# One value tile's load cut by partitions: 112, 8 and 8 rows in place of 128

## The chip, the cores and the metric

The kernel runs on one core of a Trainium2 chip. The metric is the device time of one execution in microseconds (us), given as the median of several runs; lower is better. The core has five engines that run side by side: TensorE (PE, with its weight loads PEld), VectorE (DVE), ScalarE (ACT), GpSimd (POOL) and SyncE (SP), which here only issues transfers. Sixteen DMA engines carry the data between the main memory (HBM) and the on-chip memory (SBUF), which has 128 partitions, called rows here.

## What is computed

One decoding step of a transformer block for four sequences: attention over a cached set of 4096 keys and values in 32 heads of 128, and a gated feed-forward part, both modulated by a conditioning vector `c`. Cut to what matters:

```python
q = (h @ wq).reshape(B, 1, 32, 128).transpose(0, 2, 1, 3)      # B = 4, one query per head
scores = einsum('bhqd,bhkd->bhqk', q, k_cache) * 128 ** -0.5   # k_cache: 4 x 32 x 4096 x 128, bf16
p = softmax(scores, axis=-1)
o = einsum('bhqk,bhkd->bhqd', p, v_cache)                      # v_cache: as k_cache
x = x + ga * (o.transpose(0, 2, 1, 3).reshape(B, 1, 4096) @ wo)
h = layernorm(x) * (1 + cb) + sb
x = x + gb * gmlp(h, w_in, w_sp, b_sp, w_out)
```

The two caches hold 134 MB each and are read once; all weights together are a few per cent of that. Each cached number is used for one query only.

## The kernel before

**Tiles.** The work on the caches is cut into NT = 32 tiles, each of one batch entry and four heads (HQ = 4). A key tile and a value tile have the same shape: 128 partitions, and in each of them 128 positions (NJ) of 128 numbers (DH), bf16. That is 32 KB a partition, contiguous in HBM (`kv_view`, L91 to L94), and 4096 KB a tile. Partition 32q + r holds a stretch of positions of head q.

**Buffers.** Key tiles have two buffers named `kt`, value tiles two named `vt`. The last value tile (index L = 31) takes a `kt` buffer and is loaded in four cuts along the positions (`TAIL`), and the last key tile in two, so that the work at the end can begin on a part of the tile. All other tiles are loaded by one DMA each. Loads are issued by SP in program order (`load`, L101); a load waits on SP until the tile that had the buffer before has been used.

**The loop** (L81 to L504), iteration i: VectorE multiplies key tile i in place by the query, in two halves (`mult`, L279); TensorE sums the products over the 128 numbers with an identity matrix into `red` (`reduce_d`, L285), and VectorE finishes the sum (`sum8`, L294). The softmax of tile i-1 (`scores`: L303 to L317, on VectorE and ScalarE) and its normalisation (`norm_r`, `norm_a`, `norm_b`: L325, L332, L345) run beside it. The product of probabilities and values for tile i-2 is `pv(i - 2)` (L354, 32 matmuls that read the whole value tile), and the output of tile i-3 is picked out of PSUM (`o_pick`, `o_cols`, `o_scale`: L362, L366, L380, L396).

**The order of loads.** The schedule is written out by hand. Before the loop SP issues `wm_sb`, `wq_sb`, key tiles 0 and 1, and value tile 0. In iteration i it issues key tile i+2 after the second half of `reduce_d(i)`, and value tile i after `pv(i - 2)`, which has just freed its buffer. Value tile 16 is thus issued in iteration 16, stands in SP's queue between key tiles 18 and 19, and is read by `pv(16)` in iteration 18. In iteration 30 SP issues the last value tile's four cuts, `win_sb` and `wout_sb`.

**The tail** (L506 to L645): the last tiles' outputs, the projection with `wo`, the layer norm (which ends in `hT2`, L562), the gate matmuls on `win_sb` (L585), the activation and the product `zz` (L601), the matmuls on `wout_sb` (L608), and the result's way out.

ScalarE issues four tiny loads on a queue of its own: `c_sb` and `x_sb` (4 partitions of 1 KB each, at the start) and the two numbers of `sp_t` (one partition each, in iteration 2).

Of the kernel before, what the change touches and what calls it, by code (L numbers as in the profile page):

```python
# [16 lines left out]
KC = 64  # L17
RD = 8
TAIL = (64, 32, 16, 16)


@with_exitstack
def kernel(
# [16 lines left out]
    nc = tc.nc  # L40
    P = 128
# [7 lines left out]
    NJ = SK * HQ // P  # L49
# [3 lines left out]
    G = 4  # L53
    assert DH == P and R == 32 and NJ % KC == 0 and KC * RD == 512 and sum(TAIL) == NJ
    assert G * HQ <= R and G * DH == 512 and NQ % G == 0
    att_scale = float(DH) ** -0.5
    LN_EPS = 1e-5
    L = NT - 1
# [32 lines left out]
    def kv_view(cache, i):  # L91
        g, b = divmod(i, B)
        v = cache[b, g * HQ:(g + 1) * HQ].rearrange("h s d -> (h s) d")
        return v.rearrange("(p n) d -> p n d", p=P)  # L94

    kts, vts = {}, {}

    def load(dst, src, cuts):
        n0 = 0
        for n in cuts:  # L100
            nc.sync.dma_start(out=dst[:, n0:n0 + n, :], in_=src[:, n0:n0 + n, :])  # L101
            n0 += n
# [6 lines left out]
    def load_v(i):  # L109

        vts[i] = kvp.tile([P, NJ, DH], BF16, name="kt" if i == L else "vt", bufs=2)
        load(vts[i], kv_view(A_v_cache, i), TAIL if i == L else (NJ,))

    load_k(0)
    load_k(1)
    load_v(0)

    ident_bf = consts.tile([P, P], BF16, name="ident_bf")
# [21 lines left out]
        out=sel32, in_=ident_f.rearrange("p (q r) -> p r q", r=R), axis=AX.X, op=ALU.add  # L140
# [10 lines left out]
    for g in range(G):  # L151
        nc.vector.tensor_reduce(out=selg[:, g:g + 1], in_=idr[:, g], axis=AX.XY, op=ALU.add)
    nc.vector.tensor_reduce(
        out=sel4, in_=ident_f.rearrange("p (c b) -> p b c", b=B), axis=AX.X, op=ALU.add
# [39 lines left out]
    def normed(pool, src, name, then=None, last=None):  # L194
# [24 lines left out]
        out=sg, in0=cx, scalar1=-60.0, scalar2=-1.0, op0=ALU.max, op1=ALU.mult  # L219
# [6 lines left out]
    def mod_cols(s0, n, dst, m0=0, blocks=False):  # L226
# [21 lines left out]
        out=hs, in0=modA[:, DJ:2 * DJ, :], scalar=1.0, in1=xn, op0=ALU.add, op1=ALU.mult  # L248
# [137 lines left out]
    def o_last(i, part):  # L386
        if part == 0:
            st[i, "op"] = psum.tile([P, 2, 2], F32, name="qps", bufs=1)
        for k in range(sum(TAIL[:part]), sum(TAIL[:part + 1])):
            nc.tensor.matmul(  # L390
# [44 lines left out]
    for i in range(NT):  # L435
# [29 lines left out]
        if i == 0:  # L465
            load_v(1)
        elif 2 <= i < L:
            load_v(i)
        if i == 2:
# [13 lines left out]
                out=wo_sb, in_=A_wo[0:hl].rearrange("(t p r) n -> p t r n", p=P, r=2)  # L483
            )
            nc.sync.dma_start(out=wo_last, in_=A_wo[hl:H * DH].rearrange("(q p) n -> p q n", p=P))
        if i == 5:
# [4 lines left out]
                out=gwT, in0=gsT, scalar1=spf[:, 0:1], scalar2=None, op0=ALU.mult  # L491
            )
            nc.vector.tensor_scalar(
                out=gsT, in0=gsT, scalar1=spf[:, 1:2], scalar2=None, op0=ALU.mult
# [34 lines left out]
    def sums():  # L529
# [22 lines left out]
        out=nv2, in0=mq2[:, 0:1], scalar=mq2[:, 0:1], in1=mq2[:, 1:2],  # L552
# [7 lines left out]
        out=hl, in0=xs, scalar=mq2[:, 0:1], in1=cbT[:, :, BL], op0=ALU.subtract, op1=ALU.mult  # L560
    )
    nc.vector.scalar_tensor_tensor(  # L562
        out=hT2[:, :, BL], in0=hl, scalar=rsl, in1=sbT[:, :, BL], op0=ALU.mult, op1=ALU.add
# [4 lines left out]
        out=x1m, in0=x1[:, :, :, None].to_broadcast([P, DJ, B, HQ]),  # L568
# [11 lines left out]
    def gate(h):  # L580
# [21 lines left out]
        out=zz.rearrange("p f g b -> p g b f"), in0=z1[:, None].to_broadcast([P, 2, B, NH]),  # L602
# [3 lines left out]
    for j in range(DJ):  # L606
# [7 lines left out]
        out=mq3, in_=ps3.rearrange("p (g b f) -> p g b f", g=2, b=B), axis=AX.X, op=ALU.add  # L614
# [4 lines left out]
        out=rs3, in0=mq3[:, 1], scalar=LN_EPS, in1=rs3, op0=ALU.add, op1=ALU.subtract  # L619
# [3 lines left out]
        out=g8[:, :, 0, :], in0=gwT.rearrange("p j b -> p b j"), scalar=-1.0,  # L623
# [6 lines left out]
        out=t3[:, :, 2, :], in0=yb[:, :, 0, :], in1=gsT.rearrange("p j b -> p b j"), op=ALU.mult  # L630
    )
    nc.vector.tensor_tensor(
        out=g8[:, :, 0:2, :], in0=g8[:, :, 0:2, :],
# [5 lines left out]
        out=tt, in_=t3.rearrange("p b g j -> p b j g"), axis=AX.X, op=ALU.add  # L639
# [36 lines left out]
```

## Time and profile before

| | |
|---|---|
| time, median of 3 runs | 670.07 us (669.81 to 670.64) |
| the profiled execution's own time | 671.33 us |
| its span, first to last instruction | 669.5 us |
| mean granted TensorE clock | 0.828 |
| busy: PE, DVE, ACT | 403.3 us (60%), 421.1 us (63%), 85.0 us (13%) |
| moved by DMA | 283.18 MB, mean 423 GB/s |
| the chain that ended last | DMA 58%, DVE 28%, PE 13% |
| DVE waiting for key tiles (L279) | 190.7 us in 29 waits, the longest 17.3 us |

The page counts an engine as busy while it executes; the chain follows the work that ended last back from the end, at each step to what released it. A load's time is told from its issue on SP to its landing, so waiting in the queue behind earlier loads is part of it: 22.6 us for a key tile in the median, 30.3 us for a value tile. A load has landed when its semaphore has had sixteen increments, which the trace keeps one by one. It also keeps the single packets that the DMA engines moved, with queue, size, start and duration, but not the number of the DMA engine.

### The profile page before, as it was taken

The page shows a single profiled execution, that of the slowest core. Times are in us where ns is not written, and L with a number is a line of the kernel's source. Part 1 is how long each engine was busy: PE and PEld are TensorE (multiplying, and loading weights), DVE is VectorE, ACT ScalarE, POOL GpSimd, SP SyncE. Part 2 cuts the span into 40 slices and gives each one's busy share as a digit, 9 for nine tenths or more (in the row PEclk, how much of TensorE's full clock was granted, in tenths as well). Part 3 has the DMA queues.
Part 4 walks back from the last instruction along what each step waited for, and adds up shares of the span by engine and source line. Part 5 has one row for each costly group of instructions (what it writes and reads, how often), then busy time and mean ns, then how long its engine had stood idle before and what let it go on. Part 6 is the DMA issues. An engine that isn't in the chain of part 4 may idle for free.

```text
span 669.5 us, 7043 instructions
## 1 busy us (share of the span) xinstructions
PE 403.3 (60%) x2920; PEld 181.8 (27%) x2920; DVE 421.1 (63%) x614; ACT 85.0 (13%) x278; POOL 3.8 (1%) x17
## 2 busy tenths in 40 slices
PE   1185886365676576557655664675565467555666
PEld 1032432122232232223222222232222233222325
DVE  3186494765666776666677665567766666776833
ACT  1011111110111111001111100111111011111112
POOL 1000000000000000000000000000000000000000
PEclk9999877678888777898877689878778897877975
DMA  9999999999999999999999999999999999999994
GB/s 376 437 426 435 400 404 418 433 439 428 430 433 434 435 432 431 432 435 434 430 433 431 434 434 433 430 431 432 437 432 435 426 436 433 435 434 422 435 422 198
DMA packets 13555, 283.18 MB, mean 423 GB/s; under 512 B 1228, under 2 KB 2644, under 8 KB 4692
## 3 DMA queue, kind: packets, MB, share of 16 engines
q1 hardware_dynamic: 13504, 282.73, 98.6%
q8 instruction: 23, 0.38, 0.2%
q14 instruction: 8, 0.07, 0.0%
q10 hardware_dynamic: 20, 0.01, 0.0%
HBM read 282.73 MB, written 0.00 MB: 422 GB/s over the span
## 4 chain that ended last, share of the span: by engine, by line
DMA 58%; DVE 28%; PE 13%; issue 1%; SPq 0%; ACT 0%; DVEq 0%
DMA kt<-in_A_k_cache_dram 52%; DVE kt L279 20%; PE red L285 11%; DMA win_sb<-in_B_w_in_dram 5%; DVE osb L366 2%; DVE S L294 1%; DVE osb L362 1%; DVE mrow L303 1%; PE ops L354 1%; DVE rz L345 1%; DVE mt L307 0%; PE qps L265 0%; DVE nM L309 0%; DVE mb L305 0%; DVE nM L310 0%
## 5 line engine op out<-in xcount | busy, mean ns | idle before, releaser
L285 PE MATMUL red<-kt,ident_bf 128*128 128x512 bf16 x1024 | 302.3, 461 | 234.7 <-DVE kt L279 234.7
L279 DVE TENSOR_TENSOR kt<-kt,qbc 128x8192 bf16<-128x8192 bf16 x64 | 282.8, 4420 | 191.7 <-DMA kt<-in_A_k_cache_dram 190.7
L285 PEld LDWEIGHTS <-ident_bf 128*128 128x128 bf16 x1024 | 116.3, 114 | 408.7 <-issue 284.9
L317 ACT ACTIVATE pbd<-S,nM 32x128 bf16<-32x128 f32 x128 | 73.8, 576 | 504.9 <-DVE nM L310 463.6
L354 PE MATMUL ops<-vt,pbd 128*16 128x512 bf16 x992 | 60.7, 387 | 0.2 <-DMA vt<-in_A_v_cache_dram 0.2
L294 DVE TENSOR_REDUCE S<-red 128x64 f32<-128x512 f32 x64 | 43.7, 682 | 6.3 <-PE red L285 6.3
L366 DVE SCALAR_TENSOR_TENSOR osb<-ops,selg,osb 128x128 f32<-128x128 f32 x93 | 32.6, 351 | 3.3
L317 ACT ACTIVATION_READ_ACCUMULATOR pbd<-S,nM 32x1 f32 x128 | 32.0, 250 | 0.0
L354 PEld LDWEIGHTS <-pbd 128*16 128x16 bf16 x992 | 22.5, 90 | 23.4 <-issue 1.8
L265 PE MATMUL qps<-wq_sb,hTb 128*32 128x512 bf16 x128 | 9.2, 412 | 9.2 <-DMA wq_sb<-in_A_wq_dram 8.5
L332 PEld LDWEIGHTS sm<-rsb,ones_f 128*128 128x128 f32 x64 | 12.3, 194 | 4.5
L362 DVE TENSOR_SCALAR osb<-ops,selg 128x128 f32<-128x128 f32 x31 | 10.8, 348 | 4.3 <-PE ops L354 3.6
L380 PEld LDWEIGHTS sm<-sel,osb 128*64 128x64 f32 x224 | 9.2, 138 | 11.9 <-issue 11.4
L380 PE MATMUL sm<-sel,osb 128*64 128x2 f32 x224 | 11.6, 205 | 0.0
L269 ACT CAST qbc<-qps 128x512 bf16<-128x512 f32 x8 | 4.7, 586 | 48.3 <-PE qps L265 48.3
L303 DVE TENSOR_REDUCE mrow<-S 128x1 f32<-128x128 f32 x32 | 9.2, 286 | 1.1
L345 DVE RECIPROCAL rz<-sm 64x2 f32<-64x2 f32 x56 | 9.1, 163 | 0.4
L332 PE MATMUL sm<-rsb,ones_f 128*128 128x4 f32 x64 | 9.3, 215 | 0.0
L325 DVE TENSOR_SCALAR rsb<-mask,rs 128x4 f32<-128x4 f32 x32 | 7.1, 223 | 2.4 <-ACT pbd L317 2.4
L307 DVE STREAM_TRANSPOSE mt<-mb 128x32 f32<-128x32 f32 x32 | 6.8, 212 | 1.1
L265 PEld LDWEIGHTS <-hTb 128*32 128x32 bf16 x128 | 3.0, 99 | 13.3 <-issue 10.6
L309 DVE TENSOR_REDUCE nM<-mt 128x1 f32<-128x32 f32 x32 | 6.0, 186 | 1.1
(125 smaller groups left out, 84.4 us busy)
## 6 DMA issues: line engine op xcount, KB each, us to landing
kt<-in_A_k_cache_dram SPq DMA_DIRECT2D x31, 4096.0 KB, 22.6
vt<-in_A_v_cache_dram SPq DMA_DIRECT2D x31, 4096.0 KB, 30.3
wq_sb<-in_A_wq_dram SPq DMA_DIRECT2D x1, 4096.0 KB
kt<-in_A_k_cache_dram SPq DMA_DIRECT2D x2, 2048.0 KB, 20.3
wo_sb<-in_A_wo_dram SPq DMA_DIRECT2D x1, 3584.0 KB, 29.3
wm_sb<-in_w_mod_dram SPq DMA_DIRECT2D x1, 3072.0 KB, 10.4
kt<-in_A_v_cache_dram SPq DMA_DIRECT2D x1, 2048.0 KB
win_sb<-in_B_w_in_dram SPq DMA_DIRECT2D x1, 1792.0 KB, 33.9
```

Of the source, the lines that this page charges most:

```text
L265: nc.tensor.matmul(qp[R * q:R * (q + 1)], lhsT=hTb[:, k, b, :], rhs=wq_v[:, k, gs, q, :], start=(k == 0), stop=(k == DJ - 1), tile_positio ...
L279: nc.vector.tensor_tensor(out=kt, in0=kt, in1=bc(qbc[:, g, b, :], KC), op=ALU.mult)
L285: nc.tensor.matmul(red, lhsT=ident_bf, rhs=kt[:, :, m * RD:(m + 1) * RD], start=(m == 0), stop=(m == DH // RD - 1),)
L294: nc.vector.tensor_reduce(out=st[i, "S"][:, kc * KC:(kc + 1) * KC], in_=st.pop((i, "red", kc)), axis=AX.X, op=ALU.add,)
L303: nc.vector.tensor_reduce(out=mrow, in_=S, axis=AX.X, op=ALU.max)
L317: nc.scalar.activation(out=pbd[r, :, q], in_=S[r, :], func=AF.Exp, bias=nM[r, :], scale=att_scale, accum_out=rs[r, :],)
L332: nc.tensor.matmul(z, lhsT=ones_f, rhs=st.pop((i, "rsb")), start=True, stop=True)
L345: nc.vector.reciprocal(out=rz[h, 0, :], in_=z[h, a:HQ:2])
L354: nc.tensor.matmul(opss[i % 2][g:g + G * HQ], lhsT=pbds[i % 3][:, n, :], rhs=vts[i][:, n, :], start=(m < 4), stop=(m >= NJ // G - 4), tile ...
L362: nc.vector.tensor_scalar(out=osb, in0=ops[:, 0, :], scalar1=selg[:, 0:1], scalar2=None, op0=ALU.mult)
L366: nc.vector.scalar_tensor_tensor(out=osb, in0=ops[:, g, :], scalar=selg[:, g:g + 1], in1=osb, op0=ALU.mult, op1=ALU.add,)
L380: nc.tensor.matmul(op[64 * a:64 * (a + 1), r, :], lhsT=osb[:, r:P:2], rhs=sel4[:, a:HQ:2], start=True, stop=True, tile_position=(0, 64 * a),)
```

## The change

`load_v` gets a case for the tiles in a new list `FEW`, which holds tile 16 alone. That tile is loaded by three DMAs in place of one: partitions 0 to 111, 112 to 119, and 120 to 127, in this order, on the same queue and at the same place. Buffer, source, bytes, and all that reads the tile are as before.

```diff
 TAIL = (64, 32, 16, 16)
+
+FEW = (16,)
...
     def load_v(i):
 
         vts[i] = kvp.tile([P, NJ, DH], BF16, name="kt" if i == L else "vt", bufs=2)
-        load(vts[i], kv_view(A_v_cache, i), TAIL if i == L else (NJ,))
+        src = kv_view(A_v_cache, i)
+        if i in FEW:
+            for p0, p1 in ((0, P - 16), (P - 16, P - 8), (P - 8, P)):
+                nc.sync.dma_start(out=vts[i][p0:p1], in_=src[p0:p1])
+        else:
+            load(vts[i], src, TAIL if i == L else (NJ,))
```

## The prediction

> **What bounds the kernel now.** I read the page from the top: the slices, then the DMA queues, then the chain that ended last, and after that the timeline around the changed tile and at the end.
>
> ```profile
> DMA  9999999999999999999999999999999999999994
> ...
> q1 hardware_dynamic: 13504, 282.73, 98.6%
> q8 instruction: 23, 0.38, 0.2%
> q14 instruction: 8, 0.07, 0.0%
> q10 hardware_dynamic: 20, 0.01, 0.0%
> ```
>
> The transfer engines are full in 39 of 40 slices, and one queue, SP's (q1), fills 98.6% of them. 8.39 MB (a key and a value tile of 4096 KB each) at the 432 GB/s of the middle slices take 19.4 us. A tile has 128 rows of 32 KB, and the trace records sixteen arrivals for a load, one for each transfer engine, so an engine moves 8 rows in 9.7 us: 1.21 us a row. The trace's packet records say the same: 8,064 packets of 32 KB, the median 1.213 us. That time holds also where few engines are still at work, so it is an engine's own pace and not a share of a common one.
>
> The chain in order of time shows how this sets the end:
>
> ```profile
> 370.50 23.16 DMA kt<-in_A_k_cache_dram
> 393.69 4.42 DVE kt L279
> ...
> 628.08 33.87 DMA win_sb<-in_B_w_in_dram
> 662.00 1.67 PE red L585 x56
> ```
>
> Every iteration waits for its key tile, and the tail waits for `win_sb`. The compute between fits inside the 19.4 us: VectorE is busy 63%, TensorE 60%. So what counts is when the slowest of the sixteen engines is done.
>
> They are not done together. For `win_sb` the trace has the first arrival at 655.97 us and the others, after it, at 0.0, 0.7, 0.9, 1.3, 2.2, 2.8, 3.1, 3.2, 4.2, 4.4, 4.5, 4.5, 4.9, 5.7 and 6.0 us: eight early engines within 3.1 us, eight late ones up to 6.0. At 49 us the spread was 1.8, at 364 us (value tile 15) 3.1, at 404 us (value tile 17) 4.3. Following each engine by its packets, one 1.21 us after the other, shows why: the 23 instruction fetches of q8 (16 KB each) fall in turn on eight of the engines, and one of them sets its engine back by about 1.4 us (at 42.8 us the packets expected at 42.82 and 44.03 start at 43.77 and 45.45). 23 x 1.4 / 8 = 4 us for each of these eight by the end. The queue is never empty after 111 us, so no engine catches up.
>
> In the tail three loads release the work, all of them by their last arrival:
>
> ```profile
> 657.44 0.51 PEld L390 LDWEIGHTS <-kt 128*128 128x128 bf16 x16 [0.72 <-DMA kt<-in_A_v_cache_dram]
> ...
> 662.00 1.66 PE L585 MATMUL red<-hT,win_sb 128*128 128x4 bf16 x56 [0.68 <-DMA win_sb<-in_B_w_in_dram]
> ...
> 664.35 0.82 PEld L608 LDWEIGHTS <-wout_sb 128*128 128x128 bf16 x28 [0.36 <-DMA wout_sb<-in_B_w_out_dram]
> ```
>
> The computed inputs of the latter two are there at 661.43 (L562) and 664.33 (L601), within 0.6 us of the loads. If the latest engine moves by some time, all three loads do, and the end moves by it in full, both ways.
>
> **The change, part by part.** *Removed:* one issue of 4096 KB, 0.33 us on SP, 8 rows for each engine. *Added:* an issue with 112 rows, which I take as 7 a engine (7 x 16), and two with 8 rows. *Moved:* nothing; the three stand in the place of the one.
>
> ```profile
> 353.15 0.33 SPq L101 DMA_DIRECT2D vt<-in_A_v_cache_dram  x1
> ...
> 370.50 0.33 SPq L101 DMA_DIRECT2D kt<-in_A_k_cache_dram  x1
> ...
> 390.96 1.90 PE L354 MATMUL ops<-vt,pbd 128*16 128x512 bf16 x32
> ...
> 393.69 4.42 DVE L279 TENSOR_TENSOR kt<-kt,qbc 128x8192 bf16<-128x8192 bf16 x1 [6.17 <-DMA kt<-in_A_k_cache_dram]
> ```
>
> *Issues.* Two more at 0.33 us make 0.66 us on SP. SP's next issue is 17 us later and waits for other engines, so 0; without that cover 0.66 us.
>
> *Waits.* The product at L354 waits for three loads in place of one. Tile 16's arrivals cannot be told apart; halfway between those of tiles 15 and 17 its last would be at 384.2, 6.8 us before 390.96. Behind that product on TensorE stands the reduction of the next key tile, which needs the multiply from 393.69 to 398.1; behind it on SP, the load of value tile 18. The product takes 1.9 us, so it may start as late as 396.2 without holding up the reduction: 12 us after the tile's usual arrival. Cost 0 under that cover; beyond it, each microsecond of lateness counts.
>
> *The rows.* This is the term that decides. The loads of `c_sb` and `x_sb` (4 rows of 1 KB) left four packets each on q10, and the two one-row loads of `sp_t` one each: a narrow load uses as many engines as it has rows. So an 8-row part should occupy eight engines with one row each; I assume the same eight for both parts. Their share of the tile is then 7 + 2 rows, that of the other eight 7. The engine that carried the `sp_t` loads and the four that carried `x_sb` show no q8 fetch while I can follow them, which puts the eight in the early group (likely, not certain).
>
> How fast 8 rows are written, the trace does not show; every large load in it fills 128 rows. Bounds for one 8-row part: at the engine's pace, 1.21 us. At the other end the rate goes with the rows filled: 432 GB/s over 128 rows is 3.4 GB/s a row, so 32 KB take 9.7 us, the same as eight rows one after another down a single engine's stream. No row lies near either end (the only narrow loads carry 1 KB rows and are over in 0.05 us a packet), so I take the middle, (1.21 + 9.68) / 2 = 5.44 us.
>
> Sum for the early group: 7 x 1.21 + 2 x 5.44 = 19.4 us in place of 9.7, that is +9.7. Its latest member was 3.1 us behind the first and becomes 12.8; the end was set at 6.0. So +6.8 us: span 676.3 for 669.5. The profiled execution took 671.33 us, 1.8 around its span; on the median of 670.07 it is **676.9 us**. With the bounds: at 1.21 us the early group ends at 3.1 + 1.2 = 4.3, the late one at 6.0 - 1.2 = 4.8, and the end comes 1.2 us earlier, 668.9; at 9.68 us a part the group loses 2 x 9.68 - 1.21 = 18.1 us, ends at 21.2, and the end is 15.2 later, 685.3.
>
> [...]
>
> **Rivals.** *Rebalancing at full pace.* Narrow parts run at 1.21 us a row; eight late engines lose a row and the early ones gain one: -1.2 us, 668.9. For it: an engine's packets take the same time whatever the others do, and the arrivals part into 8 and 8. [...]
> *Wrong side.* The parts fall on the late eight, at full pace: the latest goes from 6.0 to 7.2, +1.2 us, 671.3. This is slower by one row's time; it decides where the fetches and the narrow loads share engines. Against it stand the packets of `x_sb` and `sp_t`.
> *No shift.* The two parts take different eights, or are spread over all sixteen: each engine has 8 rows as before, 670.1. Against it: with one row to each engine, nothing suggests that the queue picks up where it left off.
>
> **How the numbers follow.** Slow narrow parts (671.5 to 685.3 around 676.9, the likeliest's own range) 0.64; rebalancing 0.27; wrong side 0.05; no shift 0.04. This kernel's measurement can tell about 0.2%, 1.3 us. Rebalancing at 1.2 us lies just inside that and falls on either side: 0.15 beyond it, 0.12 within. Faster 0.15; same 0.12 + 0.04 + 0.03 of the wrong side = 0.19; slower 0.64 + 0.02 = 0.66. The range takes in rebalancing with some noise below (668.4) and the forecast up to 683.5, where most of what lies under its bound of 685.3 is in; about 0.08 is left above and 0.03 below.
>
> **What would show it.** In the changed profile: packets of 32 KB that take several times 1.21 us around 380 to 395 us, GB/s well under 430 in that slice, the arrivals of the loads after it 9 to 13 us apart, and TensorE at L354 waiting for the value tile there. If no packet is longer and the last spread of `win_sb` is about 4.8 us, rebalancing holds and my forecast is wrong; 7.2 us is the wrong side; 6.0 no shift. A gain over 1.3 us, or a loss with unchanged arrivals, would show that I have missed a mechanism.

## The result, and the profile after

The changed kernel took 686.34 us in the median of 4 runs (684.30 to 686.94) against 669.97 before: 1.023 times the time, with a 95% interval of 1.021 to 1.025. Slower by 6.8 us was forecast; it is slower by 16.4, outside the range and past the bound of 685.3. The profiled execution took 686.27 us with a span of 684.4, 14.9 over the span before.

The time is lost in one place. The slices of the page, after:

```profile
DMA  9999999999999999999999999999999999999993
GB/s 376 439 429 434 430 402 431 429 428 429 432 443 434 432 431 428 429 432 435 440 432 355 199 372 435 435 432 435 428 430 431 436 431 432 439 432 420 435 425 157
```

A slice is 17.1 us. From 359 to 410 us three slices move 355, 199 and 372 GB/s in place of 432; no slice before or after them shows a loss like it against the kernel before. The share of the DMA engines stays at 9 throughout: they are busy, with packets that take longer. The three slices lack (77 + 233 + 60) x 17.1 = 6.3 MB, which at 432 GB/s are 14.6 us: nearly the whole loss in the span. (The loss in the median is larger, 16.4 us, because the profiled execution of the kernel before, 671.33 us, lay 1.4 us above its median.)

A finer cut, stretches of the same two kernels; the columns after the length are busy time and instructions of each engine, TensorE's clock, the DMA share and GB/s. First before, then after:

```profile
372.00:380.00 8.00, 1.57 (x11) 0.49 (x4) 5.52 (x5) 0.00 (x0) 0.00 (x0) 0.66 1.01 434
386.00:396.00 10.00, 6.09 (x66) 3.17 (x66) 3.83 (x5) 0.00 (x0) 0.00 (x0) 0.95 1.00 431
400.00:408.00 8.00, 5.80 (x30) 2.46 (x28) 6.78 (x10) 2.31 (x8) 0.00 (x0) 0.88 1.01 438
```

```profile
372.00:380.00 8.00, 0.00 (x0) 0.10 (x1) 4.11 (x1) 0.00 (x0) 0.00 (x0) 0.69 0.97 217
386.00:396.00 10.00, 4.99 (x44) 2.79 (x42) 3.04 (x4) 0.00 (x0) 0.00 (x0) 0.98 0.88 161
400.00:408.00 8.00, 3.59 (x32) 1.07 (x32) 0.00 (x0) 0.00 (x0) 0.00 (x0) 0.50 0.99 424
```

There are two slow stretches, and the trace's packets of 32 KB fit them. Up to 368 us they take 1.21 us. Those that start from 370 to 384 us, while the 112-row part is on its way, take about 2.3 us (1.7 to 2.6). Those that start from 384 to 396 us, when the two 8-row parts are under way, take 2.2 to 3.9. From 400 us on it is 1.21 again. What the packets took beyond 1.21 us, added up over the sixteen engines and divided by 16, is 7.1 us for those that start before 384 and 7.4 us for the later ones: two halves. The cut at 384 is a rough one: by the arrivals the 112-row part lands from 386.18 to 394.58 us and the two 8-row parts, eight arrivals each, from 389.88 to 399.88, so late engines are still on the wide part while early ones are on the narrow ones. What each part costs is told apart by the experiments.

The timeline after shows who waits (the multiply is now L286, the product L361, the three loads L117, other loads L103):

```profile
352.06 1.45 SPq L117 DMA_DIRECT2D vt<-in_A_v_cache_dram  x3
...
369.80 0.35 SPq L103 DMA_DIRECT2D kt<-in_A_k_cache_dram  x1
...
375.89 4.43 DVE L286 TENSOR_TENSOR kt<-kt,qbc 128x8192 bf16<-128x8192 bf16 x1 [8.99 <-DMA kt<-in_A_k_cache_dram]
...
400.01 3.59 PE L361 MATMUL ops<-vt,pbd 128*16 128x512 bf16 x32 [7.46 <-DMA vt<-in_A_v_cache_dram]
...
409.29 4.42 DVE L286 TENSOR_TENSOR kt<-kt,qbc 128x8192 bf16<-128x8192 bf16 x1 [20.25 <-DMA kt<-in_A_k_cache_dram]
```

Key tile 19, behind tile 16 in the queue, lands at 409.26 us in place of 393.67, 15.6 later, and VectorE waits 20.25 us for it in place of 6.17. In the chain of waits that one load stands for all of it:

```profile
369.80 39.47 DMA kt<-in_A_k_cache_dram
409.29 4.42 DVE kt L286
```

It was 23.16 us before. At the end `win_sb` arrives last at 676.44 us, 14.5 later. Next to nothing was caught up.

### The profile page after: what moved, and what is told of

Its sections match the earlier page's. It is cut to its first block, busy times and chain, and to the rows that moved or that the text cites. A ratio compares the mean times of both kernels' runs of the same rounds, so it can differ in the third digit from the quotient of the medians.

```text
span 684.4 us, 7047 instructions
## 1 busy us (share of the span) xinstructions
PE 415.7 (61%) x2920; PEld 185.2 (27%) x2920; DVE 421.0 (62%) x614; ACT 85.0 (12%) x278; POOL 3.8 (1%) x17
## 4 chain that ended last, share of the span: by engine, by line
DMA 53%; DVE 30%; PE 15%; issue 1%; ACT 1%; SPq 0%; DVEq 0%
DMA kt<-in_A_k_cache_dram 53%; DVE kt L286 21%; PE red L292 12%; DVE osb L373 3%; DVE S L301 2%; PE ops L361 1%; DVE osb L369 1%; DVE mrow L310 1%; DVE mt L314 1%; DVE rz L352 1%; PE qps L397 0%; DVE nM L316 0%; DVE mb L312 0%; DVE nM L317 0%; PE sm L240 0%
## 5 line engine op out<-in xcount | busy, mean ns | idle before, releaser
L292 PE MATMUL red<-kt,ident_bf 128*128 128x512 bf16 x1024 | 312.8, 474 | 231.3 <-DVE kt L286 231.3
L286 DVE TENSOR_TENSOR kt<-kt,qbc 128x8192 bf16<-128x8192 bf16 x64 | 282.8, 4420 | 207.0 <-DMA kt<-in_A_k_cache_dram 206.1
L292 PEld LDWEIGHTS <-ident_bf 128*128 128x128 bf16 x1024 | 119.2, 117 | 413.4 <-issue 293.6
L361 PE MATMUL ops<-vt,pbd 128*16 128x512 bf16 x992 | 62.4, 396 | 7.5 <-DMA vt<-in_A_v_cache_dram 7.5
L361 PEld LDWEIGHTS <-pbd 128*16 128x16 bf16 x992 | 22.6, 91 | 31.7 <-issue 10.8
```

The costliest lines, as they stand in the source:

```text
L286: nc.vector.tensor_tensor(out=kt, in0=kt, in1=bc(qbc[:, g, b, :], KC), op=ALU.mult)
L292: nc.tensor.matmul(red, lhsT=ident_bf, rhs=kt[:, :, m * RD:(m + 1) * RD], start=(m == 0), stop=(m == DH // RD - 1),)
L361: nc.tensor.matmul(opss[i % 2][g:g + G * HQ], lhsT=pbds[i % 3][:, n, :], rhs=vts[i][:, n, :], start=(m < 4), stop=(m >= NJ // G - 4), tile ...
```

## The experiments

The times stand beside runs of the kernel before on the same chip (670.0 to 670.4 us). As a second measure, closer to the place, I give when key tile 19 has landed (its sixteenth arrival; 393.67 before). In kernels that do not load all of the tile the end mixes in other things: the queue runs dry for a moment (in only8s, strided8 and narrow_low as few as 14, 12 and 14 of the sixteen engines have a packet under way between 370 and 373 us), and in the tail the gate matmuls wait for `hT2` and no longer for `win_sb`. There the landing is the better number.

The expectations weigh four theories, conjectures that the runs are to part. A: engines that write into neighbouring rows at the same time share one engine's pace, so every part that is not the plain 128 rows is slow. B: only the 8-row parts are slow. C: the number of loads costs, with their waits and semaphores. D: the source side costs, where engines read rows that lie next to each other.

**Is it the number of loads?** Three loads too, each of all 128 rows, cut along the positions:

```diff
-            for p0, p1 in ((0, P - 16), (P - 16, P - 8), (P - 8, P)):
-                nc.sync.dma_start(out=vts[i][p0:p1], in_=src[p0:p1])
+            load(vts[i], src, (112, 8, 8))
```

> Tile 16 in three loads too, but each of all 128 rows: 112, 8 and 8 positions of each. Theory A and theory B: no change, 670 +- 1. Theory C (number of loads, three waits at L354, the shifted order of semaphores): about 686, as the changed kernel.

670.33 us, ratio 1.0006 (95% interval 0.9995 to 1.0017); key tile 19 lands at 392.69. Two more issues, two more waits at the product and a shifted order of semaphores cost nothing that can be measured. Theory C is out.

**Which part costs?** First the 112 rows alone:

```diff
-            for p0, p1 in ((0, P - 16), (P - 16, P - 8), (P - 8, P)):
+            for p0, p1 in ((0, P - 16),):
...
     def pv(i):
+        if i in FEW:
+            return
```

> Tile 16 gets its first 112 rows alone; the last 16 rows are not loaded and its product (L354) is left out. Theory A (engines that write into neighbouring rows at the same time share one engine's pace, so every part that is not the plain 128 rows is slow): the 112-row part takes 2.2 to 2.4 us a row as in the changed profile, 7 rows +7.6 us, less the two rows not loaded: 674 to 678 us. Theory B (only the 8-row parts are slow, as the prediction had it): 668 to 670. Theory C (the cost comes with the number of loads, their marks and waits): 668 to 670.

680.94 us, ratio 1.016 (1.013 to 1.019), above even theory A. The stretch of this kernel:

```profile
372.00:380.00 8.00, 0.00 (x0) 0.10 (x1) 4.41 (x2) 0.00 (x0) 0.00 (x0) 0.81 0.95 213
```

Half of the 434 GB/s, with packets of 2.2 to 2.4 us (1.7 to 1.9 in places). Key tile 19 lands at 400.71; with one row less for each engine it would land at 392.5 at full pace, so this part costs 8.2 us. Of the 10.9 us at the end some 2.4 come after the last load: from `win_sb`'s last arrival to the output's issue 6.0 us pass in place of 5.2, and one of the output's sixteen arrivals is 1.6 us behind. Another 6.5 stand at `win_sb`'s arrival (668.43 for 661.95), and the remaining 2 are how far the two profiled executions lie from their medians. Theory B is out: the wide part that the prediction had at full pace is half of the loss.

Then the two 8-row parts alone, with the product left out in the same way:

> Tile 16 gets rows 112 to 119 and 120 to 127 alone; its other 112 rows are not loaded and its product is left out. At an engine's full pace all engines save 7 to 8 rows of 1.21 us and the end comes 9.7 us earlier: 660.3. [...] Theory B: the whole excess of 15 us sits here: 672 to 676. Theory C: 672 to 676.

670.82 us, ratio 1.0009 (0.9997 to 1.0022): leaving out seven eighths of a tile gained nothing, though by the expectation's sum 9.7 us were to be had at full pace (strided8_low below, at nearly full pace, gains 7.0). This lies below the 672 of B and C. Key tile 19 lands at 392.82, and from 372 to 380 us:

```profile
372.00:380.00 8.00, 1.21 (x24) 0.46 (x17) 0.23 (x1) 0.00 (x0) 0.00 (x0) 0.78 0.98 152
```

**Where do the rows have to lie?** The same bytes from the same place, but the eight rows of a part land four rows apart (the edit is shown against only8s):

```diff
-            for p0, p1 in ((P - 16, P - 8), (P - 8, P)):
-                nc.sync.dma_start(out=vts[i][p0:p1], in_=src[p0:p1])
+            for p0, s0 in ((64, P - 16), (96, P - 8)):
+                nc.sync.dma_start(out=vts[i][p0:p0 + 32:4], in_=src[s0:s0 + 8])
```

> As only8s, from the same source rows, but the eight rows of each part land four rows apart (64, 68, ..., 92 and 96, 100, ..., 124). [...] If the cost of a narrow part goes with the number of rows filled, or with where the rows are read from, or with the number of loads: the same as only8s.

667.75 us, key tile 19 at 389.05: faster than only8s by 3.1 us, but packets are still at 1.9 to 2.6 us from 371 to 376. The stretch:

```profile
372.00:380.00 8.00, 1.52 (x32) 0.60 (x21) 3.96 (x1) 0.00 (x0) 0.00 (x0) 0.78 0.91 279
```

Spreading the rows helps, but the time is not that of full pace (660.3 by the expectation of only8s). A conjecture for what is left, which no run had shown at that point: rows 64 to 127 are those into which the late engines write at the same time. That says what to try next: `((0, P - 16), (32, P - 8))` in the loop, rows 0 to 60 in steps of four.

> As strided8, from the same source rows, but the two narrow parts land on rows 0, 4, ..., 28 and 32, 36, ..., 60, which I take to be rows of the early engines themselves; strided8 wrote into rows of the late ones. Theory A (shared rows of the destination make the loss; a path is one engine's pace wide): nobody shares, all packets stay at 1.21 us, 2 to 5 us below strided8's 667.8 (not all the way to 660.3, since the queue runs dry for a while in these kernels). Theory D (the source side, eight engines reading rows that lie next to each other, makes a part of the loss): packets of 2 us and more as in strided8, and its time.

663.38 us, and key tile 19 lands at 384.64, 8.2 us before only8s. The stretch of this kernel:

```profile
372.00:380.00 8.00, 2.34 (x6) 0.94 (x7) 6.60 (x10) 0.48 (x2) 0.00 (x0) 0.81 1.00 430
```

Full rate, in two narrow parts of eight rows, beside 152 GB/s for the same bytes in neighbouring rows. From 368 to 380 us five packets of 151 are long (1.6 to 2.7 us); all five start within 2 us of an instruction fetch at 370.10 (in the kernel before two are long beside the fetches at that place), and the other 146 take 1.21 to 1.23. So neither the narrowness nor the source of these parts costs anything that shows, only where the rows land. That rows 0 to 60 go at full pace and rows 64 to 124 do not, with the step the same, fits narrow parts that run on the engines which write rows 0 to 63 in a plain load; the traces have no engine numbers, so this is inferred.

**Does the source play a part?** One plain load of 128 rows from source rows 28 KB apart; the values are then not those of the tile:

```diff
+            flat = A_v_cache[i % B, (i // B) * HQ:(i // B + 1) * HQ].rearrange("h s d -> (h s d)")
+            rows = bass.AP(tensor=flat.tensor, offset=flat.offset, ap=[[112 * DH, P], [1, NJ * DH]])
+            nc.sync.dma_start(out=vts[i].rearrange("p n d -> p (n d)"), in_=rows)
```

> Tile 16 in one plain load of 128 rows whose source rows start 28 KB apart in place of 32 (they overlap, so the values are not the tile's; the bytes moved are the same). Theory A: no change, 670 +- 1. Theory D: packets longer than 1.21 us in this tile and a later end.

670.24 us, ratio 0.9996 (0.998 to 1.001), packets at 1.21 us. Another step at the source costs a full-width load nothing, and strided8_low, with only8s's source rows, runs at full rate: theory D is out for the narrow parts. For the 112-row part no run kept the destination and changed the source, so there it is not excluded by itself.

**Is it the number of rows filled?** The whole tile in halves and in quarters, `((0, P // 2), (P // 2, P))` and `((0, 32), (32, 64), (64, 96), (96, P))` in the changed kernel's loop:

> All of tile 16 in two loads, rows 0 to 63 and 64 to 127. Theory A: sixteen engines write into the rows of eight, so packets of 2.4 us for 8 rows: 676 to 682. A rate that goes with the number of rows filled: also half, the same. Full pace: 670.

> All of tile 16 in four loads of 32 rows. [...] A rate that goes with the number of rows filled (a quarter of full): packets of 4.8 us, 694 to 699. Full pace: 670.

684.17 and 683.78 us (1.021 and 1.020); key tile 19 at 406.71 and 406.91. The stretches of half64 and of quarter32:

```profile
386.00:396.00 10.00, 4.74 (x43) 2.78 (x42) 3.56 (x4) 0.00 (x0) 0.00 (x0) 0.92 0.96 210
```

```profile
386.00:396.00 10.00, 5.85 (x47) 3.14 (x45) 3.70 (x4) 0.00 (x0) 0.00 (x0) 0.98 0.95 206
```

A load of 32 rows is about as fast as one of 64: both near half the full rate (from 372 to 380 us, 188 and 211 GB/s), most packets at 2.4 to 2.6 us. A rate that goes with the number of rows, the upper end of the prediction's bounds, would have put quarter32 ten microseconds and more behind half64. half64 lies 2 us above what was expected (676 to 682); quarter32, at 683.78, lies between full pace (670) and that rate's 694 to 699.

**Eight wide twice, or sixteen wide once?** Rows 112 to 127 in one load:

> All of tile 16 in two loads, rows 0 to 111 and rows 112 to 127. [...] If the two 8-row parts cost by their being eight wide or by their number: 681 to 683, clearly below the changed kernel.

683.47 us, ratio 1.019 (1.014 to 1.024): half a microsecond above the 681 to 683 expected if width or number counts, and the interval takes in the changed kernel's 1.023 as well, so it does not decide. Key tile 19 lands at 406.60, 2.7 us before that of the changed kernel. Its packets are long in the same two steps, 2.1 to 2.5 us to 383 us and then up to 4.1.

**Does the loss add up?** `FEW = (8, 16)`:

> Value tiles 8 and 16 both in 112, 8 and 8 rows. The loss is paid each time, since a full queue gives nothing back: +16.3 twice, 701 to 704. If a part of it were hidden by the distance between early and late engines: less than twice, below 700.

702.51 us, +32.4: twice the +16.4 of one tile. Nothing is hidden, nothing given back.

**Are only the sharing engines slow?** As only8s, onto rows 0 to 7 and 8 to 15, `((0, P - 16), (8, P - 8))` with `p0:p0 + 8`:

> As only8s, from the same source rows, but the two narrow parts land on rows 0 to 7 and 8 to 15: neighbours too, but rows of the early engines, not of the late ones. If sharing slows only those engines that write into the shared rows: the late eight, which are on key tile 19 by then, keep 1.21 us a packet beside long packets of the early eight, and key tile 19 lands 8 us or so later than in strided8_low all the same, by the early eight. If a blocked row holds up others too: no packet at 1.21 us in the stretch from 371 to 379 us, as in only8s.

667.90 us, key tile 19 at 389.17, 4.5 us behind strided8_low. The stretch of this kernel:

```profile
372.00:380.00 8.00, 0.00 (x0) 0.10 (x1) 3.97 (x1) 0.00 (x0) 0.00 (x0) 0.69 0.89 254
```

The packets that start from 370 to 376 us take 2.4 to 3.0 us, every one; in only8s those from 370 to 377 take 3.0 to 4.4, every one. Fourteen to sixteen engines are at work there and only eight of them have rows of tile 16 (by the eight arrivals of each part); the others are on key tiles 18 and 19, in narrow_low in rows that nobody shares (by the inference from the strided runs), and are as slow, 2.4 us a packet and more. If sharing is what slows the eight, it holds up engines outside it too.

## Why the prediction was wrong

**Right: what bounds the kernel, and that the loss is not caught up.** The queue stays full, the key tile behind the changed one is late, and the delay at the end (14.5 us at `win_sb`) is nearly that at key tile 19 (15.6). Also right: two more issues on SP and two more waits cost nothing (cutpos), though the three issues took 1.45 us and not the 0.99 of three single ones. Tile 16's arrivals, which the prediction put at 384.2 from its neighbours, can be read in the trace of before: sixteen, from 380.43 to 384.01. In the changed kernel the product did wait longer than its cover of 396.2, to 400.01, and that cost nothing either, because the next multiply only began at 409.29, on the late key tile.

**Right in size, by luck: the two narrow parts.** They were taken at 5.44 us each, against 1.21 at full pace: 2 x 4.23 = 8.5 us. only8s lands key tile 19 at 392.82, strided8_low at 384.64: 8.2 us. But 5.44 was the middle of two bounds, and neither bound's reason holds: quarter32 (683.78 us, not 694 to 699) speaks against a rate that goes with the rows filled, only8s (packets of 3.0 to 4.4 us) against one pace for every load. The four kernels that load the same 16 rows and nothing else of the tile show two causes of about equal size. Landing of key tile 19:

| | four rows apart | neighbours |
|---|---|---|
| within rows 0 to 63 | 384.64 (strided8_low) | 389.17 (narrow_low) |
| within rows 64 to 127 | 389.05 (strided8) | 392.82 (only8s) |

Neighbours cost 4.5 and 3.8 us, rows above 63 cost 4.4 and 3.7. The prediction had neither as such.

**Wrong: "an issue with 112 rows, which I take as 7 a engine (7 x 16)", costed at an engine's full pace.** This is the step that failed. Its seven rows took 2.2 to 2.4 us each, 8.2 us more at key tile 19 (only112), as much as the narrow parts. I had asked how fast rows are written in a load that is not the plain one for the 8-row parts alone, and said there that every large load in the trace fills 128 rows. A load of 112 rows had thus no example either, and the bounds had to be applied to all three loads. Put in, it closes the sum: 8.2 + 8.2 - 1.2 for the row that the late engines lose are 15.2 us; measured were 14.5 to 15.6 along the trace and 16.4 at the median.

**Wrong: the early engines' lead as cover.** The sum took off 2.9 us because the early eight may lose that much before they set the end. The late eight were held up in the same stretch: every packet that starts from 370 to 396 us takes 1.7 us or more, and the arrivals of key tile 19 are 6.6 us apart, not the 9 to 13 that the prediction named as its sign, so there was hardly a lead to use. Together with the 112 rows this took the result past the upper bound, which held the late engines fixed as well.

**The rivals.** Rebalancing at full pace fails on its condition: the narrow parts do not run at full pace where the tile's rows lie (no packet under 2.2 us from 384 to 396 us). That the narrow parts fall on the early eight, which it also needs, holds only in part. In strided8_low each of the second part's eight arrivals follows one of the first's by 1.19 to 1.25 us, one row, which fits the same eight engines, as assumed. Counted one row back, they match arrivals of key tile 18 that are about the 1st, 3rd, 4th, 5th, 7th, 9th, 10th and 12th of sixteen: earlier on the whole, but five of the first eight and not all. The split itself was not sharp either: the eighth and ninth arrivals of `win_sb` are 3.1 and 3.2 us after the first. Wrong side and no shift, both at full pace, are out by the packets.

**What stays open.** half64 and quarter32 agree (684.17 and 683.78 us), though a load of the one fills twice the rows of a load of the other, and the 112-row load ran at half the rate (213 GB/s in only112 from 372 to 380 us, 434 before): in these runs the rate of a part does not follow from the number of rows that it fills. Which rows each engine gets of a 112-row load no run here shows. That the 112-row part costs 8.2 us is measured; why it does stays open.

No version came out that beats both kernels. The ones below 669 us leave out work. A shift of rows from the late engines to the early ones would, by the inference from the strided runs, have to write into the late ones' rows, where strided8 was slowed (key tile 19 at 389.05, 384.64 in strided8_low); no run tried it on a full tile.

## What to carry to other kernels

A load that fills all 128 rows in one go is fast here (1.21 us for a packet of 32 KB); cut by positions it stays so (670.33 us), cut by rows it does not, even into large parts (684.17 us in halves). The runs fit the reading that in the plain load each engine writes into rows of its own, which no trace shows. Before costing such an edit, ask of every part, not only of the odd small one, whether the trace has a load of that shape; if not, the bounds go to each. And where one engine is slowed, a lead of the others is cover only if they keep their pace; here they did not (1.7 us a packet and more from 370 to 396 us).

## What the runs showed of the hardware

While eight engines write eight rows, packets of 32 KB take anything between 1.21 us (strided8_low: rows four apart in 0 to 63) and 3.0 to 4.4 us (only8s: neighbours in 112 to 127), in the same queue and with the same source. A 32-row load and a 64-row load run at about the same rate, 206 and 210 GB/s from 386 to 396 us (quarter32, half64). And engines that, as inferred, write only into rows of their own slow down with the others: 254 GB/s for all sixteen in narrow_low from 372 to 380 us, though eight of them, by the same inference, shared nothing. Where the rows landed and how fast is measured in each case; whose rows they are, and so the sharing, is a reading that fits all of them and that no run shows.
